# Order and spacing of attention's items beside a channel mixer, and the scaling of turned q on VectorE instead of GpSimd

## The chip, the core and the metric

The kernel runs on one core of a Trainium2 chip. A core has five engines with a queue of instructions each, worked off in order: TensorE (PE: matrix products, with PEld for the loading of weights), VectorE (DVE), ScalarE (ACT), GpSimd (POOL) and SyncE (SP), whose queue issues most of the transfers here. Engines wait for each other by semaphores. The metric is the device time of one execution in microseconds (us); lower is better. A profile of one execution is shown beside the times.

## What is computed

q, k and v have 8 batches of 12 heads, 448 tokens and 64 features. Attention with RMS-normed q and k gives x (448 x 768 for each batch); a low-rank mixing over tokens and a two-layer mixer over channels follow.

```python
def rmsnorm(x, g):
    rms = np.sqrt(np.mean(x * x, axis=-1, keepdims=True) + 1e-06)
    return x / rms * g
q_n, k_n = (rmsnorm(q, g_q), rmsnorm(k, g_k))
scores = (1.0 / np.sqrt(64)) * np.matmul(q_n, k_n.transpose(0, 1, 3, 2))
attn = np.exp(scores - np.max(scores, axis=-1, keepdims=True))
attn = attn / (np.sum(attn, axis=-1, keepdims=True) + 1e-09)
x = np.matmul(attn, v)                 # heads side by side: (8, 448, 768)
...
u = x + (x.transpose(0, 2, 1) @ U @ V).transpose(0, 2, 1)     # U: 448x32, V: 32x448
out = u + np.maximum(u @ w_ch1, 0.0) @ w_ch2                  # 768 -> 3072 -> 768
```

The output is compared in float32; the kernel multiplies in bf16.

## The kernel before, in words

Everything stays on the core. The 96 heads are handled in 24 groups of four heads (three groups to a batch), a group is two pairs of heads. The steps of a group:

- *load* brings q, k and v as float32 through SP's queue. *squares* squares q and k (ScalarE, L138, in the steady part; GpSimd in the beginning), *sums* adds the squares up for each token (VectorE, L159), *roots* turns them into 1/rms by a logarithm and an exponential (ScalarE, L165 and L166). *scale_all* runs roots, multiplies q and k by 1/rms into bf16 (GpSimd, qn and kp, L169, or L188 and L192) and copies v to bf16 (L196, L198).
- q and k are turned so that features lie on partitions. Up to group 5 this is done by TensorE (*turn*, called by *T*, L343) with VectorE copying the result and scaling q by the gains gg (*take_q*, L352; *take_k*). From group 6 on (DMA_FROM) it is done by four transposing transfers in SP's queue (*turn_dma*, L367 and L369), after which *take_dma* (L374) multiplies the whole turned q of the group, 128 partitions by 896 elements, by gg in place. The scores of a group need the scaled q.
- *Sc* computes the scores of a pair for two blocks of keys (two matmuls side by side for each of the pair's heads, L402) and takes their exponential (ScalarE, L403). For the fourth call, r = 3, both heads' last keys lie in one block, with one matmul (tile sl). *Srows* calls Sc several times in a row: "three exponentials" are three Sc calls, r = 1, 2, 3 of a group's second pair, or r = 2, 3 of its first pair with r = 0 of its second between them. The scores' PSUM pool has two buffers (ps_sc); all other PSUM tiles share four (ps).
- *V* multiplies one half of the exponentials with v (L420, L424); VectorE divides by the row sums (L427, L428) and writes x.

The mixer of a batch: *mix_t*, *mix_tr* and *mix_rows* (L441, L448, L493; VectorE casts tb at L443 and adds at L498) compute u and turn it by transfers; *up* is one of 24 products with the first weight (six matmuls, L508, then Relu on ScalarE, L510); *down* makes an output tile of 128 tokens by 384 channels from 24 matmuls, in four quarters of six (L534); after the last quarter VectorE adds u (L542) and SP stores the rows.

The order of all queues is written by hand. `att` lists attention's items with a cost each (*add_att*), `mlp` the mixer's. A loop at the end of the kernel takes from both lists: an attention item is issued as long as the sum of costs issued so far is not above what is due for the mixer's cost so far. So a cost behind an attention item says how much mixer work follows it, and items of cost 0 follow at once. From batch 1 on, `att` is filled by a loop over the pairs: `gi` is the group, `a` is 0 for its first pair and 1 for its second, `pr` is the pair within the batch. One batch of the mixer runs beside the next batch's attention. Loads are put off while *turning* is set, between mix_t and the last mix_rows.

Of the kernel before, what the change touches and what calls it, by code (L numbers as in the profile page):

```python
# [13 lines left out]
ALU = AluOpType  # L14
# [10 lines left out]
def kernel(  # L25
# [13 lines left out]
    nc = tc.nc  # L39
# [213 lines left out]
    gg = consts.tile([P, 2], FP32)  # L253
# [117 lines left out]

    def take_dma(gi):
        qT = q_bufs[gi % 2]
        nc.gpsimd.tensor_scalar(qT, qT, gg[:, 0:1], None, ALU.mult)  # L374
        for a in range(2):
            qk[(gi, a)] = [qT[:, a], kT_bufs[gi % 2][:, a]]

    def T(gi, i):
        if gi >= DMA_FROM:
            if i == 0:  # L380
                take_dma(gi)
            return
        turn(gi, i)
        for a in range(2):
            (take_q, take_k)[i](gi, a)
# [167 lines left out]
    pairs = [(b, pr) for b in range(B) for pr in range(NPAIR)]  # L553
    att = []

    def add_att(cost, f, *a):
        att.append((cost, f, a))
# [55 lines left out]
    for i, (b, pr) in enumerate(pairs):  # L613
        if b == 0:
            continue
        gi, a = divmod(i, 2)
        more = gi + 1 < len(groups)
        by_dma = gi + 1 >= DMA_FROM
        soon = gi + 2 < len(groups)

        nxt = pairs[i + 1 - a]

        if pr == 0 and b > 1:
            add_att(0.55, V, *pairs[i - 1], 0)
            add_att(0.55, V, *pairs[i - 1], 1)
        if a == 0:
            add_att(0.5, Srows, ((b, pr, 0), (b, pr, 1)))
            if i == 2 * DMA_FROM - 2:
                add_att(0.0, load, DMA_FROM + 1)
            if by_dma and more:  # L630
                add_att(0.0, scale_all, gi + 1)
            if b == 1 and pr == 0:
                add_att(0.4, lambda: None)
            if not by_dma:
                add_att(0.0, squares, gi + 1, 0, nc.gpsimd)
                add_att(0.0, squares, gi + 1, 1, nc.gpsimd)
                if gi + 2 >= DMA_FROM:
                    add_att(0.0, load, gi + 2)
            if pr != 0:
                add_att(0.55, V, *pairs[i - 1], 0)  # L640
                add_att(0.55, V, *pairs[i - 1], 1)
            add_att(0.7, Srows, ((b, pr, 2), (*nxt, 0), (b, pr, 3)))
            if not by_dma:
                add_att(0.0, sums, gi + 1, 0)
                add_att(0.0, sums, gi + 1, 1)
            if more and by_dma:
                add_att(0.0, turn_dma, gi + 1)
                add_att(0.0, take_dma, gi + 1)
                if gi + 1 == DMA_FROM:
                    add_att(0.0, weights, 2)  # L650
                if gi + 3 < len(groups):
                    add_att(0.0, load, gi + 3)
            if not by_dma:
                add_att(0.0, scale_all, gi + 1)
            add_att(0.55, V, b, pr, 0)
        else:
            add_att(0.7, Srows, ((b, pr, 1), (b, pr, 2), (b, pr, 3)))
            if more and not by_dma:
                add_att(0.39, T, gi + 1, 0)
            if soon and gi + 2 >= DMA_FROM:  # L660
                add_att(0.0, squares, gi + 2, 0)
                add_att(0.0, squares, gi + 2, 1)
            add_att(0.55, V, *pairs[i - 1], 1)
            if more and not by_dma:
                add_att(0.39, T, gi + 1, 1)
            if soon and gi + 2 >= DMA_FROM:
                add_att(0.0, sums, gi + 2, 0)
                add_att(0.0, sums, gi + 2, 1)
    add_att(0.55, V, *pairs[-1], 0)
    add_att(0.55, V, *pairs[-1], 1)  # L670

# [93 lines left out]
    while ia < len(att) or im < len(mlp):  # L765
# [6 lines left out]
        if take_att:  # L772
            c, f, a = att[ia]
# [11 lines left out]
        else:  # L785
            c, f, a, _ = mlp[im]
# [34 lines left out]
```

## Time and profile before

| what | value |
|---|---|
| median of 3 runs | 595.97 us (595.38 to 597.58) |
| the profiled execution | 596.07 us, span 594.3 us |
| mean granted TensorE clock | 0.995 |
| DMA read, written | 52.20 MB, 11.01 MB |
| last attention on TensorE | about 486 us; only mixer work behind it |

The span is what lies between the first and the last instruction of the program; some 1.8 us of the execution's time lie around it. Busy time by stretches of the span shows where TensorE is not at work. The columns are the stretch in us, then its length, and for each engine its busy time with the number of instructions; the last three are the granted clock, the share of DMA time and GB/s:

```profile
core 0: us, PE busy (x) PEld busy (x) DVE busy (x) ACT busy (x) POOL busy (x), PEclk, DMA share, GB/s
0.00:25.00 25.00, 18.57 (x249) 14.85 (x250) 16.11 (x54) 18.92 (x30) 18.46 (x30) 1.00 0.87 216
25.00:50.00 25.00, 23.79 (x248) 14.69 (x245) 18.50 (x45) 16.39 (x25) 21.77 (x25) 0.93 1.14 234
50.00:75.00 25.00, 22.60 (x208) 12.39 (x208) 12.72 (x30) 18.86 (x33) 13.92 (x13) 1.00 1.18 252
75.00:100.00 25.00, 22.16 (x225) 12.87 (x222) 11.09 (x29) 15.10 (x24) 14.70 (x23) 1.00 1.23 210
100.00:150.00 50.00, 48.58 (x396) 27.21 (x395) 15.77 (x34) 29.69 (x47) 19.80 (x31) 1.00 0.54 123
150.00:200.00 50.00, 50.00 (x441) 29.82 (x440) 18.90 (x41) 24.50 (x35) 17.14 (x25) 1.00 0.53 132
350.00:400.00 50.00, 49.27 (x429) 28.39 (x427) 19.15 (x40) 28.58 (x44) 16.43 (x25) 1.00 0.43 96
550.00:594.30 44.30, 39.30 (x235) 22.79 (x233) 4.46 (x8) 4.35 (x8) 0.00 (x0) 0.97 0.14 36
```

The stretches left out between 150 and 550 us have TensorE busy for all of their 50 us. The first 45 us (batch 0's attention, with no mixer work to put beside it) and the last five (the store of the last rows) are the same in both kernels. A matmul's record reaches past the start of the next one, so times between starts are the safer measure of TensorE's work.

### The profile page before, as it was taken

What the parts mean: (1) busy time and instruction counts of PE and PEld (TensorE: products, weight loads), DVE (VectorE), ACT (ScalarE), POOL (GpSimd) and SP (SyncE); (2) the same over time, 40 slices, a digit from 0 to 9 for tenths busy, and PEclk for the clock granted to TensorE, in tenths of its full rate; (3) what the DMA queues carried; (4) which work ended last, traced back from release to release, by engine and by line L of the source; (5) the groups of instructions that cost most, each with busy time, mean ns of one, the idle gap of its engine ahead of it and who ended that gap; (6) DMA issues with size and microseconds to landing.
All of it is one profiled execution on the core that took longest, in us unless ns stands there. A gap on an engine that the chain in (4) does not pass through costs nothing.

```text
span 594.3 us, 11608 instructions
## 1 busy us (share of the span) xinstructions
PE 574.3 (97%) x4792; PEld 333.5 (56%) x4792; DVE 196.5 (33%) x454; ACT 307.4 (52%) x482; POOL 201.9 (34%) x288
## 2 busy tenths in 40 slices
PE   8799998999999999999999999999999999999996
PEld 7554455555566555655566555565556655655563
DVE  6775544512334312621235320541234310410011
ACT  7767784467453775466753568346753254014200
POOL 6995565243153333515053514424243000000000
PEclk9899999999999999999999999999999999999999
DMA  9999999573346550693164742566015210220022
GB/s 233 200 241 239 257 193 195 118 191 72 101 90 173 146 127 16 120 238 100 36 150 99 180 106 34 147 152 175 2 34 112 50 28 0 60 68 1 0 55 53
DMA packets 104508, 68.19 MB, mean 115 GB/s; under 512 B 66568, under 2 KB 101256, under 8 KB 104456
## 3 DMA queue, kind: packets, MB, share of 16 engines
q1 hardware_dynamic: 95044, 58.03, 41.0%
q0 software_dynamic: 9408, 9.44, 9.6%
q8 instruction: 37, 0.61, 0.4%
q14 instruction: 15, 0.12, 0.1%
q10 hardware_dynamic: 4, 0.00, 0.0%
HBM read 52.20 MB, written 11.01 MB: 106 GB/s over the span
## 4 chain that ended last, share of the span: by engine, by line
PE 90%; DMA 3%; ACT 3%; POOL 1%; DVE 1%; SPq 1%; issue 1%; POOLq 0%; ACTq 0%
PE ph L508 36%; PE po L534 36%; PE pv L424 6%; PE sc L402 5%; ACT E L403 2%; PE sl L402 2%; PE pv L420 2%; PE pm L493 2%; DMA qT<-qn 1%; DMA vf<-in_v_dram 1%; POOL qT L374 1%; PE pt L343 1%; PE pu L441 1%; DVE ssq L159 1%; ACT hT L510 0%
## 5 line engine op out<-in xcount | busy, mean ns | idle before, releaser
L534 PE MATMUL po<-w2b,hT 128*128 128x384 bf16 x1344 | 238.0, 326 | 0.0
L508 PE MATMUL ph<-uT,w1b 128*128 128x448 bf16 x1140 | 229.4, 352 | 0.0
L403 ACT ACTIVATE E<-sc,gg 128x896 bf16<-128x896 f32 (+1 forms) x150 | 140.3, 990 | 120.6 <-PE sc L402 120.4
L534 PEld LDWEIGHTS <-hT 128*128 128x128 bf16 x1344 | 126.0, 98 | 77.3 <-issue 3.7
L510 ACT ACTIVATE hT<-ph 128x448 bf16<-128x448 f32 x190 | 102.1, 548 | 119.7 <-PE ph L508 118.7
L508 PEld LDWEIGHTS <-w1b 128*128 128x128 bf16 x1140 | 108.0, 98 | 95.2 <-issue 3.0
L188 POOL TENSOR_TENSOR qn<-qf,rs 128x384 bf16<-128x384 f32 x36 | 29.9, 829 | 140.5 <-ACT rs L166 137.4
L427 DVE RECIPROCAL r<-pv 128x4 f32<-128x4 f32 x96 | 17.5, 182 | 178.9 <-PE pv L424 178.5
L374 POOL TENSOR_SCALAR qT<-qT,gg 128x896 bf16<-128x896 bf16 x18 | 45.4, 2522 | 90.1 <-DMA qT<-qn 68.9
L542 DVE TENSOR_TENSOR ob<-po,x 128x384 f32<-128x384 f32 x48 | 26.7, 557 | 115.4 <-PE po L534 115.4
L424 PE MATMUL pv<-va,E 128*128 128x65 bf16 x1152 | 57.6, 194 | 0.0
L424 PEld LDWEIGHTS <-E 128*128 128x128 bf16 x1152 | 51.0, 98 | 6.3 <-issue 0.2
L402 PE MATMUL sc<-qT,kT 64*128 64x448 bf16 (+1 forms) x294 | 43.9, 356 | 7.9 <-ACT E L403 3.8
L159 DVE TENSOR_REDUCE ssq<-sq 128x14 f32<-128x896 f32 x45 | 46.7, 1077 | 3.2 <-ACT sq L138 3.1
L420 PE MATMUL pv<-vl,E 128*128 128x130 bf16 x192 | 42.4, 221 | 2.8 <-ACT E L403 2.7
L428 DVE TENSOR_TENSOR x<-pv,r 128x256 bf16<-128x256 f32 x96 | 40.8, 425 | 3.3
L402 PEld LDWEIGHTS <-kT 64*128 64x128 bf16 (+1 forms) x336 | 14.1, 94 | 46.1 <-issue 42.6
L498 DVE TENSOR_TENSOR x<-pm,x 128x384 bf16<-128x384 f32 x48 | 26.5, 554 | 23.4 <-PE pm L493 19.3
L188 POOL TENSOR_TENSOR kp<-kf,rs 128x384 bf16<-128x384 f32 x36 | 29.8, 828 | 0.0
L403 ACT ACTIVATE E<-sl,gg 128x448 bf16<-128x448 f32 x42 | 26.9, 639 | 0.0
L420 PEld LDWEIGHTS <-E 128*128 128x128 bf16 x192 | 18.8, 98 | 13.1 <-ACT E L403 5.0
L196 POOL CAST va<-vf 128x768 bf16<-128x768 f32 x24 | 20.6, 860 | 0.0
(92 smaller groups left out, 299.7 us busy)
## 6 DMA issues: line engine op xcount, KB each, us to landing
qf<-in_q_dram SPq DMA_DIRECT2D x23, 448.0 KB, 3.6
kf<-in_k_dram SPq DMA_DIRECT2D x23, 448.0 KB, 5.6
out_dram<-ob SPq DMA_DIRECT2D x50, 192.0 KB, 2.7
vf<-in_v_dram SPq DMA_DIRECT2D x48, 192.0 KB, 5.9
w1b<-in_moe_w_ch_dram POOLq DMA_DIRECT2D x4, 1152.0 KB, 18.2
w2b<-in_moe_w_ch_dram POOLq DMA_DIRECT2D x8, 576.0 KB, 14.0
vf<-in_v_dram SPq DMA_DIRECT2D x48, 32.0 KB, 4.9
out_dram<-ob SPq DMA_DIRECT2D x12, 96.0 KB, 3.4
```

The costliest lines, as they stand in the source:

```text
L159: nc.vector.tensor_reduce(ssqs[gi][:, i, :], sqs.pop((gi, i)), AX, ALU.add)
L188: nc.gpsimd.tensor_tensor(main.rearrange("p (t i) d -> p i t d", i=2), src[:, c, :2 * NJ].rearrange("p (i t) d -> p i t d", i=2), rs[:, c, ...
L374: nc.gpsimd.tensor_scalar(qT, qT, gg[:, 0:1], None, ALU.mult)
L402: nc.tensor.matmul(sc[:, i, :S], kT[d, keys], qT[d], start=True, stop=True)
L403: nc.scalar.activation(es[(b, pr)][:, 2 * r:2 * r + n, :], sc[:, :n, :S], AF.Exp, scale=scal, bias=bias)
L420: nc.tensor.matmul(pv[:, i].rearrange("p e d -> p (e d)"), E[:, 2 * NJ, w:w + P], vl[:, lp, :], start=True, stop=False)
L424: nc.tensor.matmul(pv[:, i, e, :], E[:, 2 * j + e, w:w + P], va[:, (first_h + step * e) * NJ + j, :], start=False, stop=(e == 1 and j == N ...
L428: nc.vector.tensor_tensor(xs[b].rearrange("p i (h d) -> p i h d", d=D)[:, 2 * half:2 * half + 2, h0:h0 + step + 1:step, :], pv[:, :, :, :D ...
L508: nc.tensor.matmul(ph, w1b[:, dt, ht * P:(ht + 1) * P], uT[:, dt, off:off + S], start=(dt == 0), stop=(dt == KD - 1))
L510: nc.scalar.activation(hT[:, ht, off:off + S], ph, AF.Relu)
L534: nc.tensor.matmul(po, hT[:, ht, col:col + P], w2b[:, ht, half * HALF:(half + 1) * HALF], start=(ht == 0), stop=(ht == KH - 1))
L542: nc.vector.tensor_tensor(ob[:, h], po, urows(b, col, half), ALU.add)
```

## The change

Two things are changed, both in the steady part of the kernel.

*take_dma*, the scaling of a group's turned q by gg, is issued on VectorE instead of GpSimd. It also moves in the list: it stood right behind turn_dma, in the group's first pair, ahead of a half of P·V and of the three exponentials of the second pair; now it is the last item of the second pair, behind the second pair's V and the sums of the group after next, and in front of the next group's first items.

The spacing of attention's items changes from batch 1 on. Behind the first pair's three exponentials the cost goes from 0.7 to 1.0, behind the second pair's from 0.7 to 0.6; V costs 0.4 or 0.5 instead of 0.55; the first two score items of a pair 0.45 instead of 0.5; the empty item in batch 1's first group 0.8 instead of 0.4. For the groups turned by TensorE (groups 4 and 5 here) the turn of q comes ahead of the second pair's three exponentials and the turn of k right behind them; before, the turn of q came behind these and the turn of k behind V.

```diff
     def take_dma(gi):
         qT = q_bufs[gi % 2]
-        nc.gpsimd.tensor_scalar(qT, qT, gg[:, 0:1], None, ALU.mult)
+        nc.vector.tensor_scalar(qT, qT, gg[:, 0:1], None, ALU.mult)
...
-        nxt = pairs[i + 1 - a]
-
-        if pr == 0 and b > 1:
-            add_att(0.55, V, *pairs[i - 1], 0)
-            add_att(0.55, V, *pairs[i - 1], 1)
         if a == 0:
-            add_att(0.5, Srows, ((b, pr, 0), (b, pr, 1)))
+            if pr == 0 and b > 1:
+                add_att(0.5, V, *pairs[i - 1], 0)
+                add_att(0.5, V, *pairs[i - 1], 1)
+            add_att(0.45, Srows, ((b, pr, 0), (b, pr, 1)))
...
             if b == 1 and pr == 0:
-                add_att(0.4, lambda: None)
+                add_att(0.8, lambda: None)
...
             if pr != 0:
-                add_att(0.55, V, *pairs[i - 1], 0)
-                add_att(0.55, V, *pairs[i - 1], 1)
-            add_att(0.7, Srows, ((b, pr, 2), (*nxt, 0), (b, pr, 3)))
+                add_att(0.4, V, *pairs[i - 1], 0)
+                add_att(0.5, V, *pairs[i - 1], 1)
+            add_att(1.0, Srows, ((b, pr, 2), (b, pr + 1, 0), (b, pr, 3)))
...
             if more and by_dma:
                 add_att(0.0, turn_dma, gi + 1)
-                add_att(0.0, take_dma, gi + 1)
...
-            add_att(0.55, V, b, pr, 0)
+            add_att(0.4, V, b, pr, 0)
         else:
-            add_att(0.7, Srows, ((b, pr, 1), (b, pr, 2), (b, pr, 3)))
             if more and not by_dma:
                 add_att(0.39, T, gi + 1, 0)
+            add_att(0.6, Srows, ((b, pr, 1), (b, pr, 2), (b, pr, 3)))
+            if more and not by_dma:
+                add_att(0.39, T, gi + 1, 1)
             if soon and gi + 2 >= DMA_FROM:
                 add_att(0.0, squares, gi + 2, 0)
                 add_att(0.0, squares, gi + 2, 1)
-            add_att(0.55, V, *pairs[i - 1], 1)
-            if more and not by_dma:
-                add_att(0.39, T, gi + 1, 1)
+            add_att(0.5, V, *pairs[i - 1], 1)
             if soon and gi + 2 >= DMA_FROM:
                 add_att(0.0, sums, gi + 2, 0)
                 add_att(0.0, sums, gi + 2, 1)
+            if more and by_dma:
+                add_att(0.0, take_dma, gi + 1)
```

## The prediction

> **What bounds the kernel now.** I read the page first, then TensorE's waits, the timeline around each wait, and busy time by stretch.
>
> ```profile
> span 594.3 us, 11608 instructions
> PE 574.3 (97%) x4792; PEld 333.5 (56%) x4792; DVE 196.5 (33%) x454; ACT 307.4 (52%) x482; POOL 201.9 (34%) x288
> PE sc L402 <- ACT E L403: 3.8, 8, 0.9
> PE sc L402 <- POOL qT L374: 3.2, 2, 1.8
> PE pv L420 <- ACT E L403: 2.7, 3, 1.0
> PE pw L448 <- DVE tb L443: 0.7, 1, 0.7
> ```
>
> TensorE works without a pause for 97% of the span; what is to be won is only its waits. Each wait below is counted from start to start, some 0.15 more than the profile's idle time. A product of the first mixer weight ("up") takes 1.14 us (102 matmuls in 19.29), a quarter of the second ("quarter") 0.975 (192 in 31.21), four score matmuls 0.49, with the fifth 0.69, one half of P·V 0.49, one row of the mixer 0.17. After 42 us, waits stand at 50.28 (0.53), 53.03 (0.95), 61.06 (0.61), 69.23 (1.04), 84.41 (1.19), 94.01 (1.9), 114.33 (1.5) and 376.48 (0.9): 8.6 us. More than that can't be gained.
>
> **What goes.** Five of them lie in batch 1 (0.53+0.95+0.61+1.04+1.19 = 4.3): P·V waits for the last of three exponentials, or scores for turned keys. The new order puts another up or quarter there. The waits at 94.01 and 114.33 are for GpSimd's scaling of turned q:
>
> ```profile
> L374 POOL TENSOR_SCALAR qT<-qT,gg 128x896 bf16<-128x896 bf16 x18 | 45.4, 2522 | 90.1 <-DMA qT<-qn 68.9 <-PE ph L508 13.3 <-PE po L534 7.9
> L352 DVE TENSOR_SCALAR qT<-pt,gg 128x448 bf16<-128x448 bf16 x10 | 4.0, 446 | 5.2 <-PE pt L343 5.2
> ```
>
> GpSimd is off TensorE's path in the other 16 groups, so its 45.4 us are worth nothing there.
>
> **The scaling on VectorE (d).** No row shows 128x896 on VectorE from SBUF. Bounds: 0.165 (its cheapest 128-partition instruction, a memset) and 1.08 (896 elements at one per cycle, the sum L159). Copies of turned k, 0.354 for 384 elements and 0.184 for 64, give 0.53 ns an element; 896 make 0.63. I take 0.6. The Trainium skill (VectorE: DVE Perf Modes, the perf-mode tier table) allows 4 elements a cycle for a bf16 tensor_scalar within SBUF; with its fixed 150 cycles that would be an estimated 0.39, and the sum 2.5 us less; no trace here shows it.
>
> **Where the scaling now stands.** In the order of the built kernel, VectorE has, at the end of each second pair: reciprocal and product of P·V, *the addition of the mixer item that TensorE has just finished*, the two sums of squares of the group after next (L159), the scaling, and TensorE's next instruction is the next group's first score, which waits for it. Before, GpSimd had scaled long before, and the sums held up no score. The trace shows that very queue once, with the cast of tb in the place of the scaling:
>
> ```profile
> 373.51 0.55 PE L402 MATMUL sc<-qT,kT 64*128 64x448 bf16 x4
> 373.62 0.56 DVE L542 TENSOR_TENSOR ob<-po,x 128x384 f32<-128x384 f32 x1 [1.31 <-PE po L534]
> 374.09 2.07 DVE L159 TENSOR_REDUCE ssq<-sq 128x14 f32<-128x896 f32 x2
> 376.07 0.35 DVE L443 CAST tb<-pu 128x192 bf16<-128x192 f32 x1
> 376.48 0.29 PE L448 MATMUL pw<-ident,tb 128*128 128x128 bf16 x2 [0.73 <-DVE tb L443]
> ```
>
> The addition starts 0.11 after TensorE has got to the score; the sums 0.47 later; the next instruction 1.98 after them; from the cast's end to TensorE 0.06. A score behind the scaling waits 0.11+0.47+1.98+0.6+0.06 = **3.2 us**, and the sums can't run early, because the addition ahead of them waits for TensorE.
>
> There are 18 scalings (groups 6 to 23). Where the next group opens a batch (9, 12, 15, 18, 21), two halves of P·V and some 4.5 us of mixer stand between scaling and score: no wait. Group 6 belongs to batch 1, below. The other twelve, by what stands last ahead of the score:
> - a finished quarter, groups 7, 10, 17, 19, 20, 22: 6 x 3.2 = 19.3;
> - a row of the mixer, 13: 3.25; the cast of tb, 16: 0.10+0.28+1.98+0.66 = 3.0;
> - a quarter, but no sums any more, 23: 0.11+0.47+0.66 = 1.25;
> - ups alone, 8, 11, 14: nothing blocks the sums, but ScalarE sets them:
>
> ```profile
> 129.99 0.55 PE L402 MATMUL sc<-qT,kT 64*128 64x448 bf16 x4
> 133.68 0.99 ACT L138 ACTIVATE sq<-qf 128x896 f32<-128x896 f32 x1
> 134.70 2.08 DVE L159 TENSOR_REDUCE ssq<-sq 128x14 f32<-128x896 f32 x2 [0.42 <-ACT sq L138]
> 136.94 0.36 PE L402 MATMUL sc<-qT,kT 64*128 64x448 bf16 x2
> ```
>
> With two ups behind the scores the squares start 3.7 after them, the sums end at 6.8, the scaling at 7.35; TensorE needs 0.69+2.27+0.49+2.27 = 5.7 in group 14: 1.55. In 8 and 11 a third up and its activation put the squares at 4.7 and the end at 8.35, against 6.95 of work: 1.4 each.
>
> Sum of the twelve 31.3; less the waits at 114.33 and 376.48 (2.4): +28.9. With d at its bounds 0.165 and 1.08 it is 5.2 less or 5.8 more. The transposes land earlier than the sums end: the second q transpose is issued 7 us and more of TensorE work ahead, and its data take 2.5 (median landing). Their own place in SP's queue doesn't change; GpSimd's queue no longer waits for them, so the last weight transfers that stood behind that wait are issued earlier.
>
> **Batch 1.** Turns of groups 4 and 5 now come before the second pair's scores. Of group 5, in the trace: three scores 66.21, sums 67.85 to 69.93, roots to 70.5, qn 70.61 to 72.3, turn 72.78, 6.57 after the scores. New: 0.69, a row 0.16, two ups 2.27, P·V 0.49, then the turn: TensorE is there at 3.6, while the same chain, with one more activation (0.55) ahead of the roots, has qn at about 6.4: 2.75 wait. Of group 4 the sums stand behind one more row of the mixer: added by 53.5, sums to 55.5, roots 56.1, qn 57.9; TensorE is at the turn at 55.5: 2.4. Three exponentials still hold up P·V for 1.0 and 0.5 (ScalarE has 5.5 us to do from 48.33), and group 6's first score waits about 1.1 for transposes and scaling. New 7.75, against 4.3+1.9 that go: **+1.6**, between -4 (the turns wait for nothing) and +4.
>
> **The clock.** A long pause has cost more than itself once:
>
> ```profile
> 14.85:18.27 3.42, 2.02 (x26) 1.19 (x25) 1.49 (x5) 3.42 (x5) 3.28 (x4) 1.00 0.95 258
> 21.68:25.09 3.41, 1.86 (x29) 1.26 (x29) 2.81 (x7) 3.12 (x6) 2.98 (x3) 1.00 0.48 83
> 25.09:28.51 3.42, 3.42 (x38) 2.72 (x34) 3.22 (x8) 2.51 (x4) 3.40 (x3) 0.50 1.12 214
> ```
>
> First number: length, second: TensorE busy; seventh: granted clock. A stretch with TensorE idle for 1.55 of 3.41 us was followed by 3.42 us at clock 0.50; one with 1.40 idle was not. If such stretches lie end to end (I assume it from this one), a wait of 3.2 (idle 2.9) puts 1.45 or more into one of them wherever it falls, and the half-speed stretch loses up to 1.7 us of work, on average over where it falls about 1.55. Eight long waits: 12.4; the two turns about 1. The waits of 1.2 to 1.6 stay under it. I take **+13.4**; the other bound is 0.
>
> **Sum:** 596.07 (the profiled execution: span 594.3, 1.8 around it; the median of the runs, 595.97, is 0.1 lower) + 28.9 + 1.6 + 13.4 = **640**.
>
> **Rivals.**
> 1. *The waits, without the halved clock:* 596.07+30.5 = **626.6**. For it: waits of 1.9 and 1.5 here left the clock at 1.00. Against: those left fewer than 1.4 us idle in a stretch. The Trainium skill (TensorE: Matmul & The Clock Gate, Part 1) has the clock fall after a whole idle window of some 3.4 us; waits of 3.2 would never fill one, so by it this rival is right; the stretch at 21.68, 54% busy, speaks against the rule. 0.24.
> 2. *VectorE is less late:* the sums, or the scaling, overlap what stands before them, so that the eight long waits shrink to that of the ups (1.4) and the clock holds: 626.6-8x1.8 = **612**. Against it: L159 took 0.99 start to start each time. 0.08.
> 3. *Faster:* the score never finds the scaling late, because squares and sums are done before the last mixer item ends; then all eight old waits go, and the new spacing pays: 596.1-8.6 = **587.5**. It decides at one point: the scaling must start over 0.66 us before TensorE reaches the score. Only a VectorE queue without the addition ahead of the sums could do that; that of the built kernel has it, and the ups' groups are bound by ScalarE. 0.05.
> 4. *Nothing to be seen* (fewer groups wait, old waits gone): **596**, 0.03.
>
> **How the numbers follow.** Forecast 0.60 at 640, its own range 632 to 649. To leave out no more than 2 in 10 the range takes in rival 1 and the bounds of d and batch 1: 617 to 649. 0.5% (3 us) is about what a measurement tells from no change; faster 0.05, same 0.03, slower 0.92.
>
> **What would show it.** TensorE's waits list scores <- VectorE qT with some 12 waits and about 28 us, the longest near 3; one turn <- GpSimd qn wait of over 2 us twice by 75 us; no score <- GpSimd. VectorE's scaling shows 18 times at 0.4 to 0.7. The granted clock of stretches behind the long waits is under 1. It is wrong if the scores' waits stay under 10 us together, if the additions start after the sums, or if the mean clock is still 0.995 (then rival 1).

## The result, and the profile after

The changed kernel takes 637.77 us (median of 4 runs, 634.53 to 639.53) against 596.47 (4 runs, 595.38 to 597.58) for the kernel before: a ratio of 1.0686, 95% interval 1.0633 to 1.0739. It is slower by some 41 us; the forecast was 640.

The profiled execution of the changed kernel took 634.53 us, with a span of 632.8 and a mean granted clock of 0.981 (before: 596.07, 594.3, 0.995). From its page, the span, the busy time of the engines, and the shares of the chain that ended last:

```profile
span 632.8 us, 11619 instructions
PE 584.2 (92%) x4792; PEld 337.0 (53%) x4792; DVE 204.0 (32%) x472; ACT 306.5 (48%) x482; POOL 156.4 (25%) x270
...
PE 76%; issue 7%; DVE 4%; DMA 3%; ACT 3%; POOL 3%; SPq 2%; POOLq 0%; DVEq 0%; ACTq 0%
```

GpSimd has lost its 45 us and VectorE has got 7.5 more, which is the change of engine. TensorE has the same 4792 matmuls, but 48.6 us of the span without one (594.3 - 574.3 = 20.0 before), and 9.9 us more of busy time for the same work: a lower clock. Its waits (line waited at, tile waited for; us in total, times, longest):

```profile
PE sc L402 <- DVE qT L374: 15.3, 8, 3.0
PE sc L402 <- issue: 12.2, 4, 3.0
PE pt L343 <- POOL qn L169: 4.7, 2, 2.4
...
PE sc L402 <- DMA vf<-in_v_dram: 2.8, 1, 2.8
...
PE pv L420 <- ACT E L403: 0.9, 1, 0.9
```

The first, second and fourth row together are 13 waits of scores: the forecast's twelve and group 6. Only eight carry VectorE's name; at the other five the wait sits on the weight load ahead of the matmul, and the profile puts it under "issue" or a load of v that came last. The timeline shows VectorE at those places all the same: at group 17, where the wait stands under "issue", VectorE scales at 353.96 for 0.45 us and the score starts at 354.51. Here is group 7, which carries the name (start, length, engine, line; idle time and releaser in brackets):

```profile
117.81 1.30 PE L534 MATMUL po<-w2b,hT 128*128 128x384 bf16 x7
...
119.15 0.56 DVE L542 TENSOR_TENSOR ob<-po,x 128x384 f32<-128x384 f32 x1 [1.31 <-PE po L534]
119.62 2.07 DVE L159 TENSOR_REDUCE ssq<-sq 128x14 f32<-128x896 f32 x2
...
121.61 0.44 DVE L374 TENSOR_SCALAR qT<-qT,gg 128x896 bf16<-128x896 bf16 x1
...
122.10 0.55 PE L402 MATMUL sc<-qT,kT 64*128 64x448 bf16 x4 [2.99 <-DVE qT L374]
```

TensorE could have begun the score at 118.94 (seven matmuls of 0.162 from 117.81). VectorE was idle until the last matmul of that quarter let it add; then came the two sums, then the scaling, then the score: 0.21 + 0.47 + 1.99 + 0.49 = 3.16 us from start to start. Of this 0.10 is no wait: a score that waits for nothing also starts 0.26 us, not 0.16, behind a quarter's last matmul (the median of the 55 scores that follow a quarter in the two traces). So the wait costs 3.06 us here.

The clock, by busy time in stretches of 3.41 us (columns as before: stretch, length, TensorE busy with its matmuls, ..., granted clock third from the end). The stretches are chosen so that they end where the clock falls; pairs of neighbours:

```profile
55.37:58.78 3.41, 1.08 (x11) 0.70 (x11) 0.89 (x4) 0.98 (x3) 2.67 (x2) 1.00 1.18 224
58.78:62.19 3.41, 3.41 (x13) 1.02 (x11) 0.78 (x3) 1.95 (x3) 3.35 (x6) 0.50 1.21 255
120.22:123.63 3.41, 1.53 (x11) 0.77 (x11) 1.83 (x3) 1.06 (x2) 0.00 (x0) 1.00 0.62 137
123.63:127.05 3.42, 3.42 (x35) 2.25 (x33) 0.61 (x2) 1.27 (x3) 1.98 (x4) 1.00 0.78 249
188.49:191.90 3.41, 0.78 (x8) 0.39 (x8) 2.58 (x4) 0.32 (x1) 0.00 (x0) 1.00 0.26 58
191.90:195.31 3.41, 3.41 (x15) 1.80 (x13) 1.12 (x2) 2.02 (x4) 1.22 (x3) 0.50 0.03 7
352.33:355.74 3.41, 1.23 (x9) 0.64 (x10) 2.08 (x3) 0.77 (x1) 0.00 (x0) 1.00 1.04 292
355.74:359.15 3.41, 3.41 (x24) 2.09 (x23) 0.00 (x0) 1.56 (x4) 1.68 (x3) 0.50 0.66 165
```

Behind group 10 (188.49), group 17 (352.33) and the first turn (55.37) TensorE then runs for 3.41 us at half speed; behind group 7, whose wait was as long, it does not. All six of these halved stretches behind a wait (at 58.8, 75.8, 191.9, 355.7, 403.5, 475.2) lie a whole number of 3.413 us apart. A border of that grid (120.22) cuts the 2.99 us idle at group 7 into 1.11 and 1.88; of the 3.00 idle at group 10 only 0.37 lies ahead of the border at 188.49.

So the 38.5 us between the two profiled executions: +2.0 of waits in batch 1 up to group 6's first score (2.50 and 2.55 at the two turns, 1.04 at P·V, 1.91 at group 6 and 0.2 elsewhere, against 6.2); +29.4 at the twelve scores behind it (30.5 from start to start, less some 0.1 each that a score takes without a wait too); less the 2.4 of old waits; and 10.1 of halved clock: the six halved stretches behind a wait hold 20.3 us of TensorE's busy time at half speed, of which half is lost, 1.7 a stretch. That agrees with the 9.9 us more of busy time above. The parts add up to 39.1, 0.6 too much.

### The profile page after: what moved, and what is told of

It is laid out like the page before. It is cut to its first block, busy times and chain, and to the rows that moved or that the text cites. A ratio compares the mean times of both kernels' runs of the same rounds, so it can differ in the third digit from the quotient of the medians.

```text
span 632.8 us, 11619 instructions
## 1 busy us (share of the span) xinstructions
PE 584.2 (92%) x4792; PEld 337.0 (53%) x4792; DVE 204.0 (32%) x472; ACT 306.5 (48%) x482; POOL 156.4 (25%) x270
## 4 chain that ended last, share of the span: by engine, by line
PE 76%; issue 7%; DVE 4%; DMA 3%; ACT 3%; POOL 3%; SPq 2%; POOLq 0%; DVEq 0%; ACTq 0%
PE po L534 32%; PE ph L508 29%; PE sc L402 5%; PE pv L424 4%; DVE ssq L159 2%; ACT E L403 2%; PE sl L402 2%; PE pm L493 1%; PE pv L420 1%; DMA qT<-qn 1%; POOL sq L140 1%; DMA vf<-in_v_dram 1%; SPq L108 1%; DMA qf<-in_q_dram 1%; PE pu L441 1%
## 5 line engine op out<-in xcount | busy, mean ns | idle before, releaser
L534 PE MATMUL po<-w2b,hT 128*128 128x384 bf16 x1344 | 243.3, 331 | 0.0
L534 PEld LDWEIGHTS <-hT 128*128 128x128 bf16 x1344 | 127.7, 99 | 80.4 <-issue 8.1
L542 DVE TENSOR_TENSOR ob<-po,u_rest 128x384 f32<-128x384 f32 x8 | 4.5, 556 | 47.2 <-PE po L534 47.2
```

The lines of the kernel that those rows point to most:

```text
L534: nc.tensor.matmul(po, hT[:, ht, col:col + P], w2b[:, ht, half * HALF:(half + 1) * HALF], start=(ht == 0), stop=(ht == KH - 1))
L542: nc.vector.tensor_tensor(ob[:, h], po, urows(b, col, half), ALU.add)
```

## The experiments

Three theories stood at the beginning. *Q*: VectorE's order of work costs the time; the scaling stands behind an addition that waits for TensorE, and behind two sums. *P*: the late place costs it, on any engine. *S*: the new spacing costs it, whatever scales q. Where a ratio is given it is to the kernel before on the same chip, with its 95% interval. The first expectations take 30.5 us for the twelve waits and 5.3 for the clock behind them, counted from start to start; 29.4 and 6.7 (four halved stretches) is the better split.

**GpSimd in the new place.** The changed kernel with one word undone:

```diff
-        nc.vector.tensor_scalar(qT, qT, gg[:, 0:1], None, ALU.mult)
+        nc.gpsimd.tensor_scalar(qT, qT, gg[:, 0:1], None, ALU.mult)
```

> The changed kernel with the scaling of turned q given back to GpSimd; its late place in the list and the new spacing stay. Theory Q (the scores wait because the scaling stands in VectorE's queue behind an addition that waits for TensorE and behind two sums): GpSimd has nothing of that kind in its queue, so the twelve waits (30.5 us) and the clock they cost in the profiled execution (5.3 us) go; group 6's first score waits some 2 us longer (2.52 against 0.45 of scaling). 634.5-30.5-5.3+2 = 601, between 597 and 604. Rival P (the late place is to blame, whatever engine): a slower engine at the same place is no better, 634 or more. Rival S (the new order of TensorE's items is to blame): about 636.

Measured: 607.02 us (605.19 to 611.15), 1.0176 (1.0132 to 1.0219). That is 31 us less than the change, with the scaling in the same place and 2.5 us instead of 0.45 long. P falls, and S can hold for some 11 us only. It came out 3 us above the forecast's upper end, and the waits say where:

```profile
PE sc L402 <- POOL qT L374: 6.7, 3, 4.0
PE pt L343 <- POOL qn L169: 5.1, 3, 2.4
```

The turns wait as in the change (2.50 and 2.55 start to start), group 6 waits 4.1 for the longer scaling, and two halved stretches follow it. GpSimd stood idle for 2.6 to 13 us ahead of each scaling late in the list, in 16 of 18 cases for the transposes, so its short queue lets it begin as soon as they land.

**The spacing alone.** As above, with the scaling right behind the transposes again; nothing of the first half of the change is left:

```diff
                 add_att(0.0, turn_dma, gi + 1)
+                add_att(0.0, take_dma, gi + 1)
...
-            if more and by_dma:
-                add_att(0.0, take_dma, gi + 1)
```

> The new spacing and order alone: the scaling is on GpSimd right behind the transposes, as before. Theory Q: no score waits for VectorE; left are batch 1's waits for turned q of groups 4 and 5 (2.5 each, with a halved clock behind them) against 4.3 us of old waits that go, and waits of 1 to 4 us for GpSimd in groups 6 and 7: about 602, between 597 and 606. Rival S: about 636.

Measured: 607.73 us (605.68 to 608.99), 1.0175 (1.0141 to 1.021); a little above its range too; it lies 0.7 above the run before it and inside its spread, so the place on GpSimd is worth nothing that can be seen. The new spacing alone costs 11 us, in the turns of batch 1 and in group 6 (4.13, with the halved clock behind it).

**The scaling alone.** The kernel before, its spacing untouched, with the scaling on VectorE as last item of the second pair:

```diff
-        nc.gpsimd.tensor_scalar(qT, qT, gg[:, 0:1], None, ALU.mult)
+        nc.vector.tensor_scalar(qT, qT, gg[:, 0:1], None, ALU.mult)
...
                 add_att(0.0, turn_dma, gi + 1)
-                add_att(0.0, take_dma, gi + 1)
...
                 add_att(0.0, sums, gi + 2, 1)
+            if more and by_dma:
+                add_att(0.0, take_dma, gi + 1)
```

> The kernel before with the scaling alone changed: on VectorE, last item of the second pair; old spacing, old order of turns. Theory Q, by what stands ahead of each score in the built order: 3.2 us in groups 10, 17, 19, 20 and 22, 3.0 in 16, 2.2 in 13 (a quarter stands between the mixer row and the score), 1.4 in 11 and 14, 1.3 in 7, 1.2 in 23, 0.4 in 8: 26.9, less the old waits at groups 7 and 376 us (2.4) and about 1 at group 6: 619.5, and 5 to 8 for halved clocks: 626, between 620 and 632. Rival S (the new order of the items makes the loss, the scaling only with it): under 605.

Measured: 624.90 us (624.61 to 625.41), 1.0464 (1.0431 to 1.0498), 1 us from the forecast. The waits behind VectorE are there without the new spacing:

```profile
PE sc L402 <- issue: 12.2, 4, 3.0
PE sc L402 <- DVE qT L374: 10.8, 7, 3.0
```

Group 10 waits 3.16 and groups 17, 19, 20 and 22 wait 3.21 each, as in the change; groups 7 and 13, which here have other mixer work ahead of the score, 1.58 and 2.18. The two halves, 28.6 and 11.4, add up to 40.0; together they cost 41.3.

**The scaling ahead of the sums.** The changed kernel with two items exchanged, so that only the two sums leave the path:

```diff
+            if more and by_dma:
+                add_att(0.0, take_dma, gi + 1)
             if soon and gi + 2 >= DMA_FROM:
                 add_att(0.0, sums, gi + 2, 0)
                 add_att(0.0, sums, gi + 2, 1)
-            if more and by_dma:
-                add_att(0.0, take_dma, gi + 1)
```

> The changed kernel with the scaling one step earlier, ahead of the two sums, still on VectorE. Theory Q: groups 7, 10, 13, 17, 19, 20, 22 and 23 keep 0.11+0.47+0.45+0.16 = 1.2 us of wait each, 16 about 1.0, the groups 8, 11, 14 nothing: 10.6 in place of 30.5, and no halved clock behind them. 634.5-30.5+10.6-5.3 = 609, between 605 and 613. Rival D (the scaling is late because the transposes land late): the sums are no part of the wait, about 636. Rival S: about 636.

Measured: 607.72 us (606.62 to 609.08), 1.0179 (1.0154 to 1.0204). Group 7 again, in this kernel's timeline:

```profile
117.90 0.56 DVE L542 TENSOR_TENSOR ob<-po,x 128x384 f32<-128x384 f32 x1 [1.31 <-PE po L534]
118.37 0.44 DVE L374 TENSOR_SCALAR qT<-qT,gg 128x896 bf16<-128x896 bf16 x1
118.73 2.07 DVE L159 TENSOR_REDUCE ssq<-sq 128x14 f32<-128x896 f32 x2
118.87 0.55 PE L402 MATMUL sc<-qT,kT 64*128 64x448 bf16 x4 [1.01 <-DVE qT L374]
```

The addition still waits for TensorE, but the sums now run beside the scores. Waits of 3.16 to 3.21 become 1.17 to 1.22 (0.21 + 0.47 + 0.50), those of groups 8, 11 and 14, which the squares had set, are gone, and none of these places is followed by a halved stretch any more. Two items exchanged are worth 30 us: what changed is Q's order of work alone. About 20 us of it are shorter waits (10.6 instead of 30.5 at the twelve scores); the rest is the clock.

**Work in the long waits.** The changed kernel with 40 matmuls of no use ahead of each of the eight scores that wait longest:

```diff
+                if gi + 1 in (7, 10, 13, 16, 17, 19, 20, 22):
+                    add_att(0.0, keep_busy, 40)
```

> The changed kernel with 40 matmuls on the identity (2.24 us, results unused) ahead of the first score of groups 7, 10, 13, 16, 17, 19, 20 and 22, that is within the eight long waits. Theory C (a stretch of 3.41 us in which TensorE is idle for about half is followed by one at half clock): the waits stay 3.2 us long, but no half-speed stretch follows them; only those behind the two turns in batch 1 are left. 634.5-5.3 = 629 for an execution like the profiled one, 627 to 631, and the runs lie closer together than the 5 us (634.5 to 639.5) of the changed kernel. Rival: the halving has another cause, or the matmuls get in the way: 634 to 640, mean clock still 0.973 to 0.981.

Measured: 625.73 us (625.38 to 625.86), 1.0478 (1.0458 to 1.0499). The wait is as long as ever, only filled; VectorE's part of the timeline around group 7 is the change's, 2.3 us earlier (38 of the 40 matmuls fall into the stretch shown):

```profile
116.79 2.28 PE L235 MATMUL busy<-ident 128*128 128x128 bf16 x38
116.88 0.56 DVE L542 TENSOR_TENSOR ob<-po,x 128x384 f32<-128x384 f32 x1 [1.31 <-PE po L534]
...
119.34 0.44 DVE L374 TENSOR_SCALAR qT<-qT,gg 128x896 bf16<-128x896 bf16 x1
119.83 0.55 PE L402 MATMUL sc<-qT,kT 64*128 64x448 bf16 x4 [0.76 <-DVE qT L374]
```

With TensorE occupied, no halved stretch is left behind group 6 (one is left in all, behind the second turn), the mean clock is 0.996, and more work takes 12 us less time. Four runs lie within 0.5 us, where the change's lie within 5: what differed from run to run was the clock.

**VectorE in the old place.** The kernel before with the engine's name exchanged and nothing moved:

```diff
-        nc.gpsimd.tensor_scalar(qT, qT, gg[:, 0:1], None, ALU.mult)
+        nc.vector.tensor_scalar(qT, qT, gg[:, 0:1], None, ALU.mult)
```

> The kernel before with the scaling on VectorE and nothing else: it stands right behind the transposing transfers, ahead of a half of P.V. If the engine itself is what costs (work on VectorE instead of GpSimd), the scaling of 0.45 us there costs next to nothing and the time is 596 or a little less (589 to 597), since GpSimd's two late scalings are gone. If VectorE's order is what costs, it now stands waiting for the transposes (some 3 to 6 us per group) with P.V's results and the mixer's additions behind it, and TensorE runs out of PSUM tiles: some 2 us for most of 17 groups and halved clock behind some: 620 us (605 to 640), waits named po or ph <- DVE.

Measured: 634.65 us (633.46 to 637.19), 1.0632 (1.0603 to 1.066), more than the 620 that I expected, and some 9 us worse than the late place with the same spacing. The dearest wait, around group 7:

```profile
112.57 0.45 DVE L374 TENSOR_SCALAR qT<-qT,gg 128x896 bf16<-128x896 bf16 x1 [7.68 <-DMA qT<-qn]
112.94 0.18 DVE L427 RECIPROCAL r<-pv 128x4 f32<-128x4 f32 x1
113.15 0.42 DVE L428 TENSOR_TENSOR x<-pv,r 128x256 bf16<-128x256 f32 x1
...
113.63 0.55 PE L402 MATMUL sl<-qT,kT 128*128 128x448 bf16 x1 [6.38 <-DVE x L428]
```

VectorE stands for 7.7 us before a transfer that has not landed, P·V's results stay in PSUM behind it, and TensorE has no tile to write to: 6.4 us at this one place, and 37 in all waits of that kernel. There were fewer waits than the "most of 17 groups" of the expectation, but much longer ones. GpSimd could afford to stand there, because little that anyone waits for comes behind it: in the kernel before, it was idle for 90.1 us ahead of its 18 scalings, and TensorE waited for two of them.

**Between the two places.** If one place is too early for the transposes and the other too late for the score, VectorE should do best right behind the second pair's scores: the transposes have had a half of P·V, some mixer work and the scores to land, and the addition that waits for TensorE is still to come. First with the spacing of the change and the turns in the old order (v1), then with the spacing of before (v2), then v1 with the new turns (v3). The edit of v2:

```diff
-                add_att(0.0, take_dma, gi + 1)
...
             add_att(0.7, Srows, ((b, pr, 1), (b, pr, 2), (b, pr, 3)))
+            if more and by_dma:
+                add_att(0.0, take_dma, gi + 1)
```

> The new spacing, with the scaling on VectorE right behind the second pair's scores (ahead of its squares, P.V and sums) and the turns of groups 4 and 5 in the old order. Theory Q: no addition that waits for TensorE late in the second pair and no sum stands ahead of the scaling, so no score waits for it; without the two turn waits batch 1 keeps one wait of 1.0 behind three exponentials and one of up to 1.5 at group 6: 596.4-8.6+2.5 = 590, between 588 and 594: faster than both kernels. Rival: VectorE then waits for the transposes in the scaling, and P.V's results and PSUM buffers behind it are late: 594 to 600.

> The kernel before with the scaling on VectorE right behind the second pair's scores; spacing and turns as before. Theory Q: GpSimd's two waits (1.9 and 1.5) go, the others stay: 596.4-3.4 = 593, between 592 and 595. Rival: VectorE stands still for the transposes with P.V's results behind it: 596 or more.

> As v1_early_old_turns, but with the turns of groups 4 and 5 in the new order. Theory T (turns ahead of the second pair's scores come before GpSimd has scaled q): 2.5 us of wait twice, and one or two halved clocks of 1.4 behind them: 590+5+2 = 597, between 595 and 600, that is 5 to 8 more than v1. Rival: the turn waits only take the place of others: as v1.

Measured: v1 595.66 us (595.2 to 597.67; 0.9981, 0.9964 to 0.9998), v2 594.04 (593.06 to 597.04; 0.9957, 0.9938 to 0.9976), v3 600.72 (600.04 to 604.08; 1.0069, 1.0048 to 1.0091). The new order of the turns costs 5.1 by itself (v3 less v1): waits of 2.50 and 2.55 instead of 0.58 and 0.63, and a halved stretch behind each. The expectation of v1 missed by 6 us, most of it one wait of 3.2 and the halved stretch behind it:

```profile
92.10 0.45 DVE L374 TENSOR_SCALAR qT<-qT,gg 128x896 bf16<-128x896 bf16 x1 [6.47 <-DMA qT<-qn]
92.47 0.17 DVE L427 RECIPROCAL r<-pv 128x4 f32<-128x4 f32 x1
92.68 0.42 DVE L428 TENSOR_TENSOR x<-pv,r 128x256 bf16<-128x256 f32 x1
...
93.16 2.00 PE L534 MATMUL po<-w2b,hT 128*128 128x384 bf16 x6 [3.02 <-DVE x L428]
```

Group 6's transposes land late (the loads beside them may be why; no run shows it), and VectorE stands there as in the run before this one. So group 6 alone was put last in the second pair (v4 is v1 with that):

```diff
-            if more and by_dma:
+            if more and gi + 1 > DMA_FROM:
                 add_att(0.0, take_dma, gi + 1)
...
+            if more and gi + 1 == DMA_FROM:
+                add_att(0.0, take_dma, gi + 1)
```

> The changed kernel with the turns in the old order and the scaling on VectorE right behind the second pair's scores, but for group 6, where it stays the last item of the second pair. With all groups early it took 595.66: there VectorE stood in group 6's scaling until the transposes had landed, P.V's results behind it, and TensorE waited 3.19 us at 93 us with a stretch of halved clock behind it. If that is the place of the loss: less 3.2 and some 1.5 of halved clock, and group 6's first score waits some 1.2 for the sums instead (1.15 to 1.9 in the other runs): 592.3 us (591 to 594), under the kernel before and under the 594.04 of the old spacing. Rival: the wait only moves to the score or to the next halved stretch: 595 to 596.

Measured: 593.85 us (592.43 to 594.45), 0.9936 (0.9915 to 0.9957). It is faster than the kernel before, by 3.4 us; against v2 it can't be told apart. Its waits for the scaling:

```profile
PE sc L402 <- DVE qT L374: 2.4, 2, 1.7
```

One is group 6's (1.82 start to start; I had expected 1.2), one group 7's (0.88), where VectorE scaled at 113.25 as soon as the transposes landed.

## Why the prediction was right

**The place and the number of waits.** Twelve scores wait for VectorE, in the groups named, and none for GpSimd; the groups that open a batch don't wait. Counted as the forecast counts, from where a score would have started, they are 29.4 us against 31.3: 3.06 to 3.11 in seven groups (predicted 3.2 and 3.25), 2.9 in group 16 (3.0), 1.08 in group 23 (1.25), 1.25 in groups 8, 11 and 14 (1.4, 1.4 and 1.55). (The forecast's terms for group 14 give 1.65, not 1.55; with that they add up to its 31.3.) The mechanism is shown by three runs: taking the sums out of the way takes 2.0 from each long wait, moving the scaling to GpSimd takes the waits away but for a few, and the scaling alone brings them.

**The scaling's own length.** Taken as 0.6, measured 0.45, 18 times. The Trainium skill (VectorE: DVE Perf Modes, the perf-mode tier table) was nearer with the estimate of 0.39 worked out from it. The 0.15 takes 1.8 us from the twelve waits, nearly all of the 1.9 by which they came out shorter. The lower bound, 0.165, is not VectorE's cheapest instruction on 128 partitions, as the forecast has it: a memset of 128x1 took 0.06. Nothing hung on it.

**Batch 1.** +1.6 predicted, +2.0 measured. Both turns wait as forecast (2.50 and 2.55 against 2.4 and 2.75); group 6 waits 1.9, not 1.1. That the turns cost more through the clock was put at 1; it was 3.4, a halved stretch behind each.

**The clock: the term that was mis-sized.** Of all terms, this was the one most off: 13.4 predicted, 10.1 measured in the profiled execution, 6.7 of it behind the long waits. The step that failed is "a wait of 3.2 (idle 2.9) puts 1.45 or more into one of them wherever it falls", and with it "eight long waits: 12.4". The level of 1.45 was read from one stretch at 21.7 us, before the steady part, and behind 42 us it doesn't hold. There, stretches with 1.53 and 1.43 of 3.41 us busy (1.9 and 2.0 idle) kept the clock. With about 2.05 us of idle time needed inside one stretch, a wait with 3.0 idle has it for (3.41 - 2.05 + 3.0 - 2.05) / 3.41 = 68% of its possible places in the grid, 5 of 8; in the profiled execution it was 4 of 8, and two turns, at some 1.7 us each. By their clocks and spans (0.979, 0.973 and 0.973; 634.6, 637.7 and 637.4), at 1.71 us lost to the clock for a stretch, the other three executions had about 8, 10 and 10 halved stretches where the profiled one had 7 (one of them, at 24.6, also in the kernel before). Their times fit: 1.9, 5.0 and 4.6 us over the profiled one's, that is about one and three stretches more. The profiled execution's sum is 596.07 + 29.4 - 2.4 + 2.0 + 10.1 = 635.2, against 634.53. That the median came within 2.3 us of 640 is luck in part: in the profiled execution only half of the long waits halve the clock, but the turns cost more than was put on them, and the other executions have more halved stretches.

**The rivals.** The first (waits without the halved clock, 626.6) is not what the kernel does, but close to what it would do: with work in the long waits, and one halved stretch left, it took 625.7. The second (VectorE less late) and the fourth fall with the waits measured. The third named its point rightly: "only a VectorE queue without the addition ahead of the sums could do that". With the scaling ahead of that addition, VectorE is worth having (594.0 and 593.9), though not the 8.6 us that were put as the most that could be won: v2 keeps the five waits of batch 1, and v4 has other ones there.

What stays open: how much of v4's gain is the new spacing's, since v2 and v4 overlap; and whether other executions of the changed kernel have their halved stretches at other groups, which only one trace shows.

## What to carry to other kernels

An instruction moved to a faster engine takes its place in that engine's order: look at what stands ahead of it there and what *that* waits for, not at its length; here 0.45 us cost up to 3.1 a time behind an addition and two sums, and exchanging two items took 30 us off. The place must be late enough for its own input and early enough for its reader, and it can differ for one group out of 18. A wait of TensorE's is dearer than its length once it leaves most of a 3.41 us stretch idle; filling it with useless matmuls shows what the clock's part is.

## What the runs showed of the hardware

The granted clock goes by a grid of 3.413 us, and what counts is how busy TensorE is in one piece of it. Behind 42 us, in the traces of all twelve kernels cut along that grid, every stretch with up to 1.30 us of TensorE work was followed by a halved one, and every one at full clock with 1.42 or more was not. The Trainium skill (TensorE: Matmul & The Clock Gate, Part 1) has such a free-running window of about 3.4 us, which these traces bear out (the halved stretches of the change lie 34, 48, 14 and 21 windows apart from 75.8 on), and the same part says the clock falls after an idle window; here a window that was 38% busy (1.30 of 3.41 us) was enough. Before 25 us there are exceptions: in eight traces a stretch with 1.59 to 1.86 us busy was followed by a halved one (1.86 is the stretch that misled the forecast), and they are not explained.

The same waits can therefore cost different time in two runs of one kernel: the change's spread of 5 us shrank to 0.5 when its waits were filled.
